# Later loads of q and v, and two more batches mixed by seven block products, in an attention and MLP-mixer kernel on one core

## The chip, the core and the metric

The kernel runs on one core of a Trainium2 chip. TensorE (PE in the profile) does matmuls and transposes into PSUM; VectorE (DVE), ScalarE (ACT) and GpSimd (POOL) work elementwise; SyncE (SP) issues most of the transfers. Each engine works through its own queue in program order and waits on semaphores for the others. The metric is the device time of one execution in microseconds, less is better; several executions are timed and the median is given.

## What is computed

Linear attention with the feature map phi(x) = elu(x) + 1, followed by one block of an MLP mixer, for 8 batches, 8 heads, 576 positions and 64 features per head. Inputs and output are float32.

```python
q_p, k_p = phi(q), phi(k)                      # phi(x) = min(exp(x), max(x + 1, 1))
kv  = einsum('bhsd,bhse->bhde', k_p, v)
z   = sum(k_p, axis=2)
x   = (q_p @ kv) / (q_p @ z + 1e-6)            # laid out as (batch, 576, 512)
h   = relu(x^T @ w_tok1) @ w_tok2              # mixing of positions, 576 -> 256 -> 576
u   = x + h^T
out = u + relu(u @ w_ch1) @ w_ch2              # mixing of channels, 512 -> 1536 -> 512
```

## The kernel before

Everything is in bfloat16 between the float32 inputs and the float32 output. Positions of a batch are split into four blocks of 128 and a tail of 64; the tails of two batches are worked on together. The order of all instructions is written by hand. It is a pipeline over batches: while batch n is mixed by channel on TensorE, batch n + 1 goes through attention and the mixing of positions, and batch n + 2 is loaded and mapped by phi. This text calls the loop pass for batch n **stage n**.

A stage is a list `big` of TensorE's pieces and a list `fill` of everything else. `put(s, fn, ...)` says that `fn` is emitted right after piece number s; what has the same s comes in the order of the `put`s. So s sets the place of an operation in the queue of its engine, and with that all that stands behind it there.

In stages 2 to 6, `big` has these pieces:

- pieces 0 to 11, the first mixing of batch n (u @ w_ch1). `mm3(n, mc)` computes one block of 128 of the 1536 hidden channels for all 512 positions: four matmuls of 512 columns (L543), and ScalarE applies relu (L550) into `cr`. There are twelve blocks. Where n is in `MIXED`, four of the twelve blocks (4, 5, 10 and 11) are computed together by a Winograd form of block multiplication, `mix_one` (L713): seven products i = 1 to 7, each four matmuls of 256 columns (L723). Their left sides are sums of weights made once (`swc`), their right sides four differences of blocks of u made by VectorE in `u_sums` (L700, into `tuc`, which is the space of `crt`). Three products are copied out of PSUM by ScalarE (L731), one has relu by ScalarE (L729), and three are finished by VectorE, which adds a copied part and clips at zero (`add_relu`, L531). The pieces are then four `mm3`, three pieces with one product and one `mm3`, products 7, 2 and 3, the last `mm3`, and product 4. `both` and `m3x` write this list.
- in stage 3 only, three pieces for the tails of batches 2 and 3 (`mm3_tail`, L557), which read `uTt`.
- fourteen pieces of the second mixing, `pair_product` (L823), also by seven products, in the order 1, 2, 6, 5, 7, 3, 4, two pieces each. They use three PSUM banks: X (products 1, 6, 7, 4), Y (5, 3) and Z (2). VectorE makes their sums of rows (`row_sums`, L666), ScalarE copies banks out in between (`pair_copy`, L828), VectorE adds u to a bank (`pair_end`, L832), and GpSimd adds the copied part and writes the result to memory.

`b0` is the number of the first of these fourteen pieces: 12, and 15 in stage 3. The rest of a stage lies between:

- `nd` for batch n + 1 at piece 1: 40 small matmuls of `qT` with `kv` (L261), then about 4.1 us of VectorE, which divides them (L270 to L289) and leaves x. `mm1` at 7 (L312) and `mm2a`, `mm2b` at 13 and b0 + 3 (L325) are the mixing of positions; VectorE's L337 makes u from them.
- `uta` and `utb` (`utr_dma`, L521): two transposes by DMA from SyncE's queue, u to `uT`, which the first mixing of batch n + 1 reads from its first matmul on. `utt` (L526) does it for a pair of tails, `ut` to `uTt`.
- phi for batch n + 2: `phi_exp` (L151, ScalarE), `phi_add` (L157, VectorE) and `phi_end` (L165, VectorE), each in two halves, once for k and once for q. `qtr_dma` (L221) then transposes q's map by two DMAs to `qT`, which `nd` of the next stage reads.
- `vcast` (L176), `kv` (L191) for batch n + 2, and `load_all(n + 3, ...)` (L132): loads of 576 KB each, two for q, two for k and two for v, into the one buffer that these have. A load waits in SyncE's queue until the old content has been read, and what stands behind it there waits too.

Stage 1 is written out by itself ahead of the loop, with pieces 0 to 31: the first mixing of batch 1 and of the tails of batches 0 and 1, its second mixing by `pair_product`, and last the second mixing of those tails (L583). In it the loads of batch 4 stand at 16 (q) and 25 (k, v), the transposes of u of batch 2 at 19 and 24.

Of the kernel before, what the change touches and what calls it, by code (L numbers as in the profile page):

```python
# [19 lines left out]
def kernel(  # L20
# [22 lines left out]
    B, H, S, D = q.shape  # L43
# [586 lines left out]
    def bf(nm, b, i):  # L630
        t = raw[nm, b].rearrange("p j f -> p (j f)").bitcast(BF16)
        return t[:, 1536 * i:1536 * (i + 1)]
# [64 lines left out]
    def u_sums(which, tu=tu, b=1):  # L697
# [5 lines left out]
    tuc = [t.rearrange("p (r j c) -> p r j c", r=2, j=2) for t in [  # L703
        crt.rearrange("p k s -> p (k s)")[:, 512 * i:512 * (i + 1)] for i in range(3)] + [
        bf("q", 1, 2)[:, 1024:1536]]]
# [159 lines left out]
    def m4s(n):  # L865
        return [lambda i=i, j=j: pair_product(n, i, j) for i in ORDER for j in range(2)]
# [133 lines left out]
    def steps(n):  # L1000

        out_ = [("kv", lambda: kv(n, range(2)))] if n < 2 else []
        if n == 1:
            puts = [nc.scalar.copy, nc.vector.tensor_copy if n == 1 else nc.scalar.copy]
            out_ += [(f"qt{c}", lambda c=c: qtr(n, c, puts[c])) for c in range(2)]
        for i, rs in enumerate(([0, 1], [2, 3], [4])) if n < 2 else ():
            for g in range(2):
                out_.append((f"nd{i}{g}", lambda g=g, rs=rs: nd(n, g, rs)))
        if n > 1:
            out_.append(("nd", lambda: nd_all(n)))  # L1010
        out_.append(("mm1", lambda: mm1(n)))
        if n > 1:
            out_ += [("mm2a", lambda: mm2(n, [0, 1])), ("mm2b", lambda: mm2(n, [2, 3]))]
            if n % 2:
                out_.append(("mm2t", lambda: mm2_tails(n // 2)))
            out_ += [("uta", lambda: utr_dma(n, [0, 1])), ("utb", lambda: utr_dma(n, [2, 3]))]
            if n % 2:
                out_.append(("utt", lambda: utr_tail_dma(n // 2)))
        return out_

    def run(bigs, fill):
        for i, big in enumerate(bigs):
            big()
            for s, fn in fill:
                if s == i:
                    fn()
        for s, fn in fill:
            assert s < len(bigs)
# [57 lines left out]
    put = lambda s, fn, *a: fill.append((s, lambda: fn(*a)))  # L1086
# [42 lines left out]
    put(24, todo["mm2b"])  # L1129
    put(24, todo["utb"])  # L1130
    put(24, pair_end, 1, "Z", 0, 0, 0)
    put(16, load_all, 4, "q")
    put(25, load_all, 4, "kv")
    put(26, pair_end, 1, "Y", 0, 1, 1)
    put(28, pair_end, 1, "X", 1, 0)
    put(28, pair_put, 1)
# [1 line left out]
    put(28, kv, 3, range(2))  # L1138
    run(big, sorted(fill, key=lambda e: e[0]))

    MIXED = (2, 3, 6)
    for n in range(2, B - 1):
        p, b = divmod(n, 2)
        tail = int(n == 3)
        mix = n in MIXED
        big = (m3x if mix else m3)(n) + m3t * tail + m4s(n) + m4(p, [8]) * tail
        b0 = 12 + 3 * tail
        todo = dict(steps(n + 1))
        fill = []
        put = lambda s, fn, *a: fill.append((s, lambda: fn(*a)))  # L1150
        at = lambda s, *nms: [put(s, todo.pop(nm)) for nm in nms if nm in todo]

        def phi_at(nm, ex, ad, en):
            for g in range(2):
                if ex is not None:
                    put(ex[g], phi_exp, nm, n + 2, 2 * g, 2)
            for g in range(2):
                put(ad[g], phi_add, nm, n + 2, 2 * g, 2)
                put(en[g], phi_end, nm, n + 2, 2 * g, 2)

        at(1, "nd")
        if n + 2 < B:
            if n > 3:
                phi_at("k", None, (2, 2), (3, 4))
                put(5, load_all, n + 3, "k")
            nm = "k" if n == 3 else "q"
            if mix:
                for which in (3, 4):
                    put(3, u_sums, which, tuc, b)
            if not mix:  # L1170
                phi_at(nm, (7, 7), (8, 9), (9, 10))
            else:
                for g in range(2):
                    put(3, phi_add, nm, n + 2, 2 * g, 2)
                    put(7, phi_exp, nm, n + 2, 2 * g, 2)
            put(10, *((qtr_dma, n + 2) if n != 3 else (load_all, n + 3, "k")))
            if n == 2:
                for g in range(2):
                    put(13, phi_add, "k", n + 2, 2 * g, 2)
        at(7, "mm1")  # L1180
        for s, k0 in ((7 if mix else 11, 0), (11 if mix else 12, 3)):
            for w in (1, 2):
                put(s, row_sums, n, w, k0, 3)
        if mix and n + 2 < B:
            for g in range(2):
                put(7 + 2 * g, phi_end, nm, n + 2, 2 * g, 2)
        if mix:
            for which in (1, 2):
                put(0, u_sums, which, tuc, b)
        if n == 3:  # L1190
            phi_at("q", (12, 13), (13, 13), (14, 14))
            put(15, qtr_dma, n + 2)
        at(13, "mm2a", "uta")
        put(14, row_sums, n, 3, 0, KH)
        put(b0 + 1, pair_copy, 0)
        if n == 2:
            for g in range(2):
                put(b0 + 1, phi_exp, "k", n + 2, 2 * g, 2)
                put(b0 + 2, phi_end, "k", n + 2, 2 * g, 2)
            put(b0 + 4, load_all, n + 3, "k")  # L1200
        at(b0 + 3 - tail, "mm2b", "utb")
        put(b0 + 4 - tail, row_sums, n, 4, 0, KH)
        put(b0 + 4 - tail, pair_end, n, "Z", 0, 0, 0)
        put(b0 + 5, pair_copy, 1)
        if n + 2 < B:
            for g in range(2):
                put(b0 + (5 if n == 2 else 2) + g, vcast, n + 2, g)
        put(b0 + 7, load_all, n + 3, "qv")
        put(b0 + 7, pair_copy, 2)
        if n > 2 and n + 3 < B:  # L1210
            put(b0 + 8, k_exp, n + 3)
        put(b0 + 9, pair_end, n, "X", 1, 1, 2)
        if n == B - 2:
            at(b0 + 6, "mm2t", "utt")
        at(b0 + 9, "mm2t")
        if n + 2 < B:
            put(b0 + 9, kv, n + 2, range(2))
        at(b0 + 9, "utt")
        put(b0 + 11, pair_end, n, "Y", 0, 1, 1)
        if n == B - 2:  # L1220
            for which in (3, 4):
                put(3, u_sums, which, tuc, b)
            put(1, first_sum)
            for which in range(1, 5):
                if which > 1:
                    put((3, 3, b0 + 2)[which - 2], first_sums, which)
                put(b0 + 10, u_sums, which)
        else:
            put(b0 + 13, pair_end, n, "X", 1, 0)
            put(b0 + 13, pair_put, n)  # L1230
        assert not todo, todo
        run(big, sorted(fill, key=lambda e: e[0]))
# [31 lines left out]
```

## Time and profile before

| | us |
|---|---|
| median of 6 executions | 252.09 |
| lowest, highest | 250.09, 254.03 |
| profiled execution | 253.14 |
| its span, first to last instruction | 251.4 |
| stage 2 (85.42 to 112.48 us of the span) | 27.1 |
| stage 3 (112.48 to 143.45) | 31.0 |
| stage 4 (143.45 to 169.11) | 25.7 |
| stage 5 (169.11 to 194.21) | 25.1 |
| stage 6 (194.21 to 218.76) | 24.6 |

A stage is counted here from its first `mm3` to that of the next. Stages 2, 3 and 6 have the seven products in their first mixing; stages 4 and 5 have not. Stage 3 has the tails of batches 2 and 3 besides.

How busy each engine is in stages 4, 5 and 6 (the columns are the stretch and its length, then busy time and number of instructions of PE, the weight loads, DVE, ACT and POOL, then the clock granted to TensorE as a share of its full speed, the mean busy share of the DMA engines, and GB/s):

```profile
143.45:169.11 25.66, 25.55 (x266) 15.96 (x266) 19.80 (x31) 16.63 (x25) 4.03 (x5) 1.00 0.76 214
169.11:194.21 25.10, 25.00 (x261) 15.84 (x262) 18.52 (x29) 14.63 (x23) 5.12 (x6) 1.00 0.53 142
194.21:218.76 24.55, 24.45 (x207) 16.54 (x207) 21.28 (x35) 9.71 (x17) 8.47 (x11) 1.00 0.34 70
```

TensorE is hardly idle in any of them. VectorE is next. Busy times of matmuls overlap, [...]so that the time between two starts is what counts: eight `mm3` matmuls of 512 columns take 1.73 us in the chain of waits, four of 256 columns 0.44 us.

### The profile page before, as it was taken

The numbers are of one execution on the slowest core, as the hardware profiler recorded it, in microseconds if no ns is written. First come the engines' busy times: TensorE is split into PE (matmuls) and PEld (weight loads), VectorE is DVE, ScalarE is ACT, GpSimd is POOL, SyncE is SP. The second block draws the span as 40 slices with busy tenths as digits, with TensorE's granted clock in tenths as the row PEclk, the third lists the DMA queues.
The fourth block names the chain that finished last, engine by engine and source line by source line (L and its number), as shares of the span: only waits on it lengthen the run. The fifth ranks groups of instructions, "written<-read, shape, count | busy, mean of one in ns | idle before, by whom it ended". The sixth has DMA issues, their size and how long they took to land.

```text
span 251.4 us, 5964 instructions
## 1 busy us (share of the span) xinstructions
PE 240.3 (96%) x2432; PEld 159.3 (63%) x2454; DVE 190.9 (76%) x330; ACT 139.4 (55%) x224; POOL 70.6 (28%) x84
## 2 busy tenths in 40 slices
PE   7899999999999699999989999999999999999994
PEld 3584455555877256775578644774478567888673
DVE  5954778897999579988986379857974888956853
ACT  4664791579765058646877268555952652175100
POOL 9770030496504500052002610052005800440000
PEclk9999999999999889999999999999999999999998
DMA  6999999999529990569959876799162602352036
GB/s 243 258 203 255 357 256 339 332 261 313 220 50 254 261 389 4 132 161 348 305 189 172 330 254 192 134 262 315 32 138 44 143 24 44 63 106 63 4 83 167
DMA packets 49771, 48.39 MB, mean 193 GB/s; under 512 B 30032, under 2 KB 35536, under 8 KB 49744
## 3 DMA queue, kind: packets, MB, share of 16 engines
q1 hardware_dynamic: 41648, 35.00, 47.3%
q0 software_dynamic: 7472, 12.22, 21.9%
q10 hardware_dynamic: 624, 0.79, 1.1%
q8 instruction: 19, 0.31, 0.5%
q14 instruction: 8, 0.07, 0.1%
HBM read 35.85 MB, written 9.44 MB: 180 GB/s over the span
## 4 chain that ended last, share of the span: by engine, by line
PE 59%; DMA 7%; DVE 3%; issue 1%; DVEq 0%
PE ps L823 18%; PE ps L543 15%; DMA uTt<-ut 5%; PE ps L751 4%; PE ps L777 4%; PE ps L312 3%; PE ps L325 3%; PE ps L723 2%; DMA uT<-u 2%; PE ps L570 2%; PE ps L592 2%; PE ps L261 1%; PE ps L191 1%; PE ps L557 1%; PE ps L583 1%
## 5 line engine op out<-in xcount | busy, mean ns | idle before, releaser
L543 PE MATMUL ps<-uT,wc 128*128 128x512 bf16 x284 | 67.7, 384 | 2.5 <-DMA uT<-u 2.1
L550 ACT ACTIVATE cr<-ps 128x512 bf16<-128x512 f32 x67 | 39.1, 600 | 37.9 <-PE ps L543 37.5
L543 PEld LDWEIGHTS <-wc 128*128 128x128 bf16 x288 | 27.5, 98 | 32.6 <-DMA uT<-u 2.6
L834 POOL TENSOR_TENSOR obuf<-obuf,q_raw 128x512 f32<-128x512 f32 x6 | 7.6, 1269 | 96.0 <-DVE obuf L832 63.4
L823 PE MATMUL ps<-k_raw,v_raw 128*128 128x256 bf16 x216 | 24.9, 273 | 0.0
L832 DVE TENSOR_TENSOR obuf<-ps,u 128x512 f32<-128x512 f32 x24 | 16.2, 686 | 10.5 <-PE ps L823 8.9
L823 PEld LDWEIGHTS <-cr 128*128 128x128 bf16 x216 | 21.0, 98 | 4.1
L823 PEld LDWEIGHTS <-v_raw 128*128 128x128 bf16 x216 | 21.1, 98 | 3.9 <-issue 0.4
L151 ACT ACTIVATE e<-q_raw 128x1152 bf16<-128x1152 f32 x16 | 18.3, 1162 | 7.2 <-DVE den L241 5.1
L151 ACT ACTIVATE e<-k_raw 128x1152 bf16<-128x1152 f32 x16 | 18.2, 1164 | 3.6 <-DMA k_raw<-in_k_dram 3.5
L823 PE MATMUL ps<-wc,cr 128*128 128x256 bf16 x144 | 17.7, 273 | 0.0
L666 DVE TENSOR_TENSOR v_raw<-cr 128x768 bf16<-128x768 bf16 (+2 forms) x24 | 14.8, 618 | 3.6 <-ACT cr L729 2.1
L276 DVE TENSOR_TENSOR x<-ps,dens 128x768 bf16<-128x768 f32 x18 | 17.2, 954 | 0.4
L337 DVE TENSOR_TENSOR u<-ps,x 128x1024 bf16<-128x1024 f32 x12 | 14.6, 1220 | 2.1 <-PE ps L325 1.9
L312 PE MATMUL ps<-x,w 128*128 128x512 bf16 x49 | 13.4, 379 | 0.3
L176 ACT CAST vs<-v_raw 128x1152 bf16<-128x1152 f32 x12 | 13.5, 1163 | 0.0
L157 DVE TENSOR_SCALAR y<-k_raw 128x1152 bf16<-128x1152 f32 x16 | 11.7, 761 | 2.2 <-DMA k_raw<-in_k_dram 2.2
L165 DVE TENSOR_TENSOR qp<-e,y 128x1152 bf16<-128x1152 bf16 x16 | 11.9, 755 | 1.0 <-ACT e L151 0.3
L157 DVE TENSOR_SCALAR y<-q_raw 128x1152 bf16<-128x1152 f32 x16 | 12.3, 783 | 0.1
L325 PE MATMUL ps<-ar,w2p 128*128 128x512 bf16 x44 | 11.8, 379 | 0.3
L834 POOL TENSOR_TENSOR obuf<-obuf,part 128x512 f32<-128x512 f32 x6 | 7.6, 1274 | 15.8 <-DVE obuf L832 15.8
L165 DVE TENSOR_TENSOR kp<-e,y 128x1152 bf16<-128x1152 bf16 x16 | 11.7, 750 | 0.5 <-ACT e L151 0.4
(178 smaller groups left out, 432.1 us busy)
## 6 DMA issues: line engine op xcount, KB each, us to landing
k_raw<-in_k_dram SPq DMA_DIRECT2D x16, 576.0 KB, 6.6
q_raw<-in_q_dram SPq DMA_DIRECT2D x16, 576.0 KB, 6.0
v_raw<-in_v_dram SPq DMA_DIRECT2D x14, 576.0 KB, 9.3
out_dram<-obuf POOLq DMA_DIRECT2D x12, 512.0 KB, 6.6
wc<-in_moe_w_ch_dram POOLq DMA_DIRECT2D x8, 384.0 KB, 10.2
out_dram<-obuf POOLq DMA_DIRECT2D x4, 256.0 KB, 5.5
cr<-in_v_dram POOLq DMA_DIRECT2D x2, 288.0 KB, 7.9
out_dram<-obuf POOLq DMA_DIRECT2D x4, 128.0 KB, 7.7
```

Of the source, the lines that this page charges most:

```text
L151: nc.scalar.activation(out=e, in_=f, func=AF.Exp)
L157: nc.vector.tensor_scalar(out=y, in0=f, scalar1=1.0, scalar2=1.0, op0=ALU.add, op1=ALU.max)
L165: live["phi"] = nc.vector.tensor_tensor(out=dst.transpose([0, 2, 1, 3]), in0=e.rearrange("p (i t d) -> p i t d", i=nj, t=T), in1=y.rearran ...
L276: nc.vector.tensor_tensor(out=xv[:, :, rc0:rc0 + 3], in0=v_[m][:, :, k0:k0 + 6, 0:D].rearrange("p i (q a) d -> p i q a d", a=2), in1=den.r ...
L312: nc.tensor.matmul(out=ps[:, mt], lhsT=w1t[:, b, ms] if r == R else w1[:, r, ms], rhs=x[b][:, r, :], start=(r == 0), stop=(r == R))
L325: nc.tensor.matmul(out=ps[:, i], lhsT=w2v(kt, r, b), rhs=ar[b][:, kt, :], start=(kt == 0), stop=(kt == NT - 1 and not add))
L543: nc.tensor.matmul(out=ps, lhsT=wc1[:, kj, 128 * mc:128 * mc + 128], rhs=uTj[b][:, kj] if n < 2 else uT[b][:, :, kj], start=(kj == 0), sto ...
L550: nc.scalar.activation(out=cr[b][:, mc, :], in_=ps, func=AF.Relu)
L666: nc.vector.tensor_tensor(out=s_[which - 1][:, ks], in0=x_, in1=y_, op=op)
L823: nc.tensor.matmul(out=live[tile_][:, j], lhsT=lhs[:, k_], rhs=rhs[:, k_], start=(first and j == 0 and k_ == 0), stop=(k_ == KH - 1), skip ...
L832: nc.vector.tensor_tensor(out=o, in0=live[tile_], in1=u[n % 2][:, d::2, HC[c]], op=ALU.add)
L834: nc.gpsimd.tensor_tensor(out=o, in0=o, in1=part[i], op=ALU.add)
```

## The change

Three places change.

- In stage 1 the load of q of batch 4 moves from piece 16 to piece 25, ahead of k and v of that batch; all six transfers now stand behind both transposes of u of batch 2 in SyncE's queue.
- In stage 2 the loads of q and v of batch 5 move from piece 19 to piece 21, behind the transpose of the tails of batches 2 and 3. In the other stages they stay.
- `MIXED` gets batches 4 and 5. In their stages the four blocks of the first mixing are computed by seven products; VectorE makes the four differences of u, two at piece 0 and two at piece 2, ahead of k's map, and the first sums of rows move to pieces 7 and 11, as in the other stages with products. In both stages q's `phi_add` and `phi_end` move from pieces 7 to 10 to pieces 17 and 18, and `qtr_dma` from 10 to 18, in SyncE's queue now behind the transposes of u and still ahead of the loads at 19. q's `phi_exp` stays at 7, k's map at 2 to 4.

For stages 2, 3 and 6 the new conditions give the same order as before, but for the load in stage 2.

```diff
@@ -1129,8 +1129,7 @@
-    put(16, load_all, 4, "q")
-    put(25, load_all, 4, "kv")
+    put(25, load_all, 4, "qkv")
@@ -1138,7 +1137,7 @@
-    MIXED = (2, 3, 6)
+    MIXED = (2, 3, 4, 5, 6)
@@ -1159,29 +1158,32 @@
         at(1, "nd")
+        if mix and 3 < n < B - 2:
+            for which in (3, 4):
+                put(2, u_sums, which, tuc, b)
         if n + 2 < B:
             if n > 3:
                 phi_at("k", None, (2, 2), (3, 4))
                 put(5, load_all, n + 3, "k")
             nm = "k" if n == 3 else "q"
-            if mix:
+            if n > 3:
+                phi_at(nm, (7, 7), (b0 + 5, b0 + 5), (b0 + 6, b0 + 6))
+            else:
                 for which in (3, 4):
                     put(3, u_sums, which, tuc, b)
-            if not mix:
-                phi_at(nm, (7, 7), (8, 9), (9, 10))
-            else:
                 for g in range(2):
                     put(3, phi_add, nm, n + 2, 2 * g, 2)
                     put(7, phi_exp, nm, n + 2, 2 * g, 2)
-            put(10, *((qtr_dma, n + 2) if n != 3 else (load_all, n + 3, "k")))
+            put(b0 + 6 if n > 3 else 10,
+                *((qtr_dma, n + 2) if n != 3 else (load_all, n + 3, "k")))
...
-        for s, k0 in ((7 if mix else 11, 0), (11 if mix else 12, 3)):
+        for s, k0 in ((7, 0), (11, 3)):
             for w in (1, 2):
                 put(s, row_sums, n, w, k0, 3)
-        if mix and n + 2 < B:
+        if n < 4:
             for g in range(2):
                 put(7 + 2 * g, phi_end, nm, n + 2, 2 * g, 2)
...
-        put(b0 + 7, load_all, n + 3, "qv")
+        if n != 2:
+            put(b0 + 7, load_all, n + 3, "qv")
...
         at(b0 + 9, "utt")
+        if n == 2:
+            put(b0 + 9, load_all, n + 3, "qv")
```

## The prediction

> **What bounds the kernel now.** I read the shares of busy time first, then the table of who waited for whom on TensorE, then the chain of waits in order of time, and last windows and timelines around the places found.
>
> ```profile
> PE 240.3 (96%) x2432; PEld 159.3 (63%) x2454; DVE 190.9 (76%) x330; ACT 139.4 (55%) x224; POOL 70.6 (28%) x84
> ```
>
> TensorE is busy for 240.3 of 251.4 us, so time goes only with matmuls, with TensorE's few idle stretches, or with a slow clock. In the waits (us in total, times, longest) only two of its idle stretches lie behind the first 20 us:
>
> ```profile
> PE ps L543 <- DMA uT<-u: 2.1, 1, 2.1
> PE ps L557 <- DMA uTt<-ut: 0.8, 1, 0.8
> ```
>
> The first stands at the seam of stage 1 and stage 2 ("stage n" is the loop in which batch n is mixed by channel). The chain in order of time (start, us, what) shows it with its sequel, and stage 5 for comparison:
>
> ```profile
> 79.31 6.06 DMA uT<-u
> 85.38 0.05 issue
> 85.42 3.10 PE ps L543 x8
> 88.52 1.12 PE ps L261 x27
> ...
> 182.50 1.31 PE ps L823 x12
> ...
> 194.21 1.73 PE ps L543 x8
> 195.94 0.72 PE ps L261 x40
> ```
>
> Stage 1's last matmul ends at 83.27; the transposes of u of batch 2 land at 85.4. Then the same eight matmuls that take 1.73 us at 194.21 take 3.10. The one-microsecond windows give the reason in their PEclk column (the one ahead of the last two):
>
> ```profile
> 84.40:85.40 1.00, 0.00 (x0) 0.00 (x0) 0.00 (x0) 0.00 (x0) 0.91 (x2) 1.00 0.98 272
> 87.40:88.40 1.00, 1.00 (x3) 0.15 (x1) 0.00 (x0) 0.05 (x1) 0.00 (x0) 0.50 1.01 336
> 89.40:90.40 1.00, 1.00 (x18) 0.52 (x13) 0.81 (x3) 0.00 (x0) 0.00 (x0) 1.00 1.02 411
> ```
>
> The clock is granted at half from about 86.0 to 89.4. SyncE's queue says why the transposes were late: 1.15 MB of q of batch 4 are issued right ahead of them.
>
> ```profile
> 75.55 1.16 SPq L132 DMA_DIRECT2D q_raw<-in_q_dram  x2
> 76.80 5.01 SPq L521 DMA_TRANSPOSE uT<-u  x2
> ```
>
> Each of these two transposes needs 2.5 us to issue and the second 6.1 to land; over all twelve the minimum and median are 3.0 and 3.1.
>
> [...]
>
> **The change, part by part.** My base is the profiled execution: 253.14 us, of which the span is 251.4.
>
> *Loads of batch 4.* All three now follow the transposes. The second transpose can issue at 79.31 as before (VectorE's L337 ends then) and lands 3.1 us later, at 82.4, 0.9 ahead of TensorE's 83.27. The wait goes: -2.15. With it goes the idleness that halved the clock. From its start to its first L823, stage 2 takes 14.72 us (85.42 to 100.14), stage 6, with the same matmuls, 13.00 (194.21 to 207.21): -1.72. Bounds: 0 to -2.15 and 0 to -1.72. What the move costs: q of batch 4 issues at about 80.6 instead of 75.6 and, at the 4.2 to 6.0 us of such loads, has landed by 87.5. VectorE reads it once nd (6.5 us into a stage) and two differences (0.8) are done, at 90.6. That cover of 3 us hides it; k and v are wanted 8 us later still.
>
> *q and v of batch 5* now follow the tail's transpose in stage 2. That issues when its data are there (about 111) behind k's 1.15 MB alone and lands, at the 6.1 us of its like, at 117 instead of 126.3; TensorE wants it at 125.5: -0.83. q and v move back about 1.2 us (one issue); q landed near 121, and its map is at 126 to 128, so 0.
>
> *Seven products in stages 4 and 5.* Sixteen 512-column matmuls (3.46 us at 216 ns) become 28 of 256 (3.05 at 109). Read from whole stages: 13.39 us from stage 5's start to its first L823 (169.11 to 182.50), 13.00 in stage 6, which has the products: -0.39 each, -0.78 together. ScalarE keeps 12 operations per stage, of 0.58 to 0.60 us each. VectorE gains four differences at 0.42 and three add-and-clip at 0.69, 3.75 us: 23.6 of 25.3 us in stage 4, 22.3 of 24.7 in stage 5. Two of the differences fit into its 1.65 us of idleness ahead of nd. The rest is tight but has a pattern: stage 2 has the products and the map of q, and its TensorE has no wait. With k's map (2.7 us) done in one piece ahead of the first add-and-clip, that ends 10.5 us into the stage and the next two at 12.2 and 12.85; the products that read them start at 13.0 and 13.65. I take 0; from nothing up to 0.5 per stage.
>
> *q's map later.* Its four operations move behind this stretch (start, us; stage 5 starts at 169.11):
>
> ```profile
> 186.88 1.23 DVE L337 TENSOR_TENSOR u<-ps,x 128x1024 bf16<-128x1024 f32 x1
> 188.03 0.95 DVE L666 TENSOR_TENSOR q_raw<-cr,v_raw 128x1536 bf16<-128x1536 bf16 x1
> 188.89 0.68 DVE L832 TENSOR_TENSOR obuf<-ps,u 128x512 f32<-128x512 f32 x1
> 190.88 0.69 DVE L832 TENSOR_TENSOR obuf<-ps,u 128x512 f32<-128x512 f32 x1 [1.31 <-PE ps L823]
> ```
>
> Their L337 waits for TensorE, which is 0.4 earlier, so the first L832 ends at 189.5 - 169.1 - 0.4 = 20.0 into the stage. The map takes 4 x 0.67 and ends at 22.75. Only then can SyncE issue the two transposes of qT, 1.4 us each, the second landing 3.6 later: 22.8 + 1.4 + 3.6 = 27.8. Before, they were issued 12 us into the stage (155.74), so nothing waited. Now nd of the next stage reads them at stage length plus 1.73: 25.27 + 1.73 = 27.0 after stage 4, 24.71 + 1.73 = 26.45 after stage 5. New waits: +0.75 and +1.3 (bounds 0.4 to 1.2 and 0.9 to 1.75, from the 4.9 to 5.4 us between the map's end and the landing in stages 2 and 3). Behind the map, the L832 that frees bank X ends at about 23.4; product 4 writes X at 23.8 in stage 4, 23.3 in stage 5: +0.1. SyncE's queue behind qT: q and v of batch 7 issue 5 us later, at 25.6; q lands 6 us on, 7 into stage 5, its exp is wanted at 8.3: 0. v is wanted at 15, the tail's transpose only in the last block: 0. GpSimd's adds shift by under 1 us and nobody waits for them.
>
> **Sum:** -2.15 - 1.72 - 0.83 - 0.78 + 0.75 + 1.3 + 0.1 = -3.33, from 253.14 to **249.8**. The profiled execution is 1.05 above the median of 252.09, and the half clock may be missing in some executions (they range over 3.9 us); the same sum from the median gives 248.8. I take **249.5**.
>
> **Rivals.**
> (a) *qT in time*: if VectorE is earlier than I think, only -5.5 remains: about 247.5. Against it: the map can't begin before the L832 at 20.0. 12%.
> (b) *One of the new waits halves the clock again*, +1.72: 251.2. For it: 2.15 us did. Against it: the 0.83 us at 125.5 left the clock at 1.00. 18%.
> (c) *Slower*: qT lands late. Its transposes share the DMA engines with q and v of batch 7 right behind them and with two 512 KB stores. The two waits sum to twice the landing minus 5.05 us; they eat up the whole gain from a landing of 5.3 us on. At the 6.1 that transposes needed behind q, the waits are 7.15, and both exceed 2.15, so twice 1.72 for the clock: 253.14 - 5.48 + 10.6 = 258.3. For it: 6.1 and 12.1 occur. Against it: in both cases the loads were ahead in the queue, here they are behind. 12%.
> (d) *The first transposes stay slow* for a reason other than q ahead of them: 253.14 - 1.61 + 2.15 = 253.7. Against it: of the other ten transposes of u nine landed in 3.0 to 3.6 us, and the one of 5.3 (at 134.8) was issued right behind those of qT, which here are done by 77.6. 8%.
>
> **Numbers.** About 1% (2.5 us) is what a measurement here can tell from no change; 1% faster is 249.57. My forecast has 50%, on its own from 248.2 to 250.8, with a little over half below 249.57. Faster: 0.30 from it, 0.12 from (a), 0.02 from (b): 0.44. Same: 0.20 + 0.16 + 0.08 = 0.44. Slower: (c), 0.12. The range reaches down past (a), to 247.2, and up past (b), to 252.4; it leaves out (c) and (d).
>
> **What would show it.** Right: SyncE issues q of batch 4 behind the two transposes, no wait of L543 for uT, PEclk at 1.00 throughout stage 2, no wait of L557; L261 waiting for DMA qT, 0.75 and 1.3 us, at the starts of stages 5 and 6; 28 matmuls of L723 in stages 4 and 5. Wrong: waits for qT over 2 us or PEclk of 0.5 behind them; waits of L823 for VectorE's L531 or L832, which would say that VectorE, not the transposes, bounds stages 4 and 5; or a wait of L157 for q of batch 4.

## The result and the profile after

| | before | after |
|---|---|---|
| median of the runs compared, us | 250.83 (70 runs) | 252.85 (33 runs) |
| lowest, highest, us | 248.11, 254.38 | 251.68, 255.04 |
| ratio, 95% interval | | 1.0092 [1.0076, 1.0108] |
| profiled execution, us | 253.14 | 252.83 |
| its span, us | 251.4 | 251.1 |

The kernel is 0.9% slower, and 252.85 lies above the forecast range, while the two profiled executions differ by 0.3 us the other way. Of 115 executions of the kernel before that ran beside the experiments below, 16 have a mean granted clock below 0.9945 and take some 2 us longer, and the profiled execution of before (0.990) is one of that kind.

TensorE in the profile after does less work and is idle for longer; the first line is that of busy times in the page, the others are from the table of who waited for whom (us in total, times, longest):

```profile
PE 237.0 (94%) x2456; PEld 160.8 (64%) x2478; DVE 199.3 (79%) x344; ACT 139.1 (55%) x224; POOL 70.9 (28%) x84
```

```profile
PE ps L261 <- DMA qT<-qp: 2.5, 2, 1.3
PE ps L823 <- DVE obuf L832: 1.6, 2, 1.1
...
PE ps L543 <- DMA uT<-u: 0.7, 1, 0.7
```

The wait for the tail's transpose is gone, the wait for u's transposes is down from 2.1 to 0.7 us. Two new ones have come, twice each: for q's transposes in front of nd, and for VectorE's add in front of the last product. Stages 4, 5 and 6 (columns as in the table before) show the bill:

```profile
139.10:165.04 25.94, 25.31 (x277) 17.15 (x278) 23.33 (x38) 16.46 (x25) 3.99 (x4) 1.00 0.51 152
165.04:192.41 27.37, 24.93 (x274) 17.09 (x274) 23.55 (x37) 14.45 (x23) 5.57 (x6) 1.00 0.61 172
192.41:218.37 25.96, 24.63 (x207) 16.61 (x207) 21.58 (x35) 9.71 (x17) 8.74 (x11) 1.00 0.39 83
```

They take 79.3 us, against 75.3 before and 76.7 by the prediction: PE's busy time shrank in stages 4 and 5, but each of the three stages grew. Where the time goes in stage 4 is seen in VectorE's timeline (start, us, instruction):

```profile
158.49 0.68 DVE L832 TENSOR_TENSOR obuf<-ps,u 128x512 f32<-128x512 f32 x1
159.09 2.49 DVE L157 TENSOR_SCALAR y<-q_raw 128x1152 bf16<-128x1152 f32 x2
161.50 1.41 DVE L165 TENSOR_TENSOR qp<-e,y 128x1152 bf16<-128x1152 bf16 x2
162.84 0.68 DVE L832 TENSOR_TENSOR obuf<-ps,u 128x512 f32<-128x512 f32 x1
```

q's map begins 20.0 us into the stage, to the tenth where the prediction put it. But its two L157 take 2.49 us instead of 1.42. GpSimd's timeline shows what stands beside them:

```profile
159.31 1.65 POOL L834 TENSOR_TENSOR obuf<-obuf,q_raw 128x512 f32<-128x512 f32 x1 [18.11 <-DVE obuf L832]
```

This add of the copied part to Z is released by the very L832 that the map follows. The kernel before has the same add at this place, with nothing of VectorE's map beside it; in its stage 5, which starts at 169.11, it is this line:

```profile
189.71 1.27 POOL L834 TENSOR_TENSOR obuf<-obuf,q_raw 128x512 f32<-128x512 f32 x1 [18.02 <-ACT w L828]
```

In the profile after, the add of stage 4 runs until 160.96, and the second L157 (the list of that line's instructions in this window gives their durations as least, median, most) takes 1.83 us:

```profile
L157 DVE TENSOR_SCALAR y<-q_raw x2: 750/1288/1827, 159.1 to 159.8; 128x1152 bf16<-128x1152 f32 x2
```

The chain of waits then goes on to the next stage: the end of the map, q's second transpose, nd. (SyncE issues the first transpose at 162.94, as soon as the map has ended; the L832 in the chain only runs meanwhile.)

```profile
162.91 0.61 DVE obuf L832
163.53 0.70 SPq L221
164.23 0.05 issue
164.28 3.83 DMA qT<-qp
168.12 0.05 issue
168.16 0.76 PE ps L261 x38
```

### The profile page after: what moved, and what is told of

It is laid out like the page before. It is cut to its first block, busy times and chain, and to the rows that moved or that the text cites. A ratio compares the mean times of both kernels' runs of the same rounds, so it can differ in the third digit from the quotient of the medians.

```text
span 251.1 us, 6016 instructions
## 1 busy us (share of the span) xinstructions
PE 237.0 (94%) x2456; PEld 160.8 (64%) x2478; DVE 199.3 (79%) x344; ACT 139.1 (55%) x224; POOL 70.9 (28%) x84
## 4 chain that ended last, share of the span: by engine, by line
PE 57%; DVE 6%; DMA 5%; issue 2%; ACT 1%; SPq 0%; DVEq 0%; ACTq 0%
PE ps L823 14%; PE ps L543 13%; PE ps L723 6%; PE ps L312 4%; PE ps L751 4%; PE ps L777 4%; PE ps L325 3%; DMA qT<-qp 3%; PE ps L570 2%; PE ps L592 2%; DMA uT<-u 2%; DVE y L157 2%; PE ps L261 1%; DVE obuf L832 1%; PE ps L557 1%
## 5 line engine op out<-in xcount | busy, mean ns | idle before, releaser
L543 PE MATMUL ps<-uT,wc 128*128 128x512 bf16 x252 | 60.2, 379 | 1.1 <-DMA uT<-u 0.7
L550 ACT ACTIVATE cr<-ps 128x512 bf16<-128x512 f32 x59 | 34.5, 600 | 39.4 <-PE ps L543 39.2
L543 PEld LDWEIGHTS <-wc 128*128 128x128 bf16 x256 | 24.2, 98 | 25.5 <-DMA uT<-u 1.2
L834 POOL TENSOR_TENSOR obuf<-obuf,q_raw 128x512 f32<-128x512 f32 x6 | 8.4, 1396 | 93.2 <-DVE obuf L832 59.1
L823 PE MATMUL ps<-k_raw,v_raw 128*128 128x256 bf16 x216 | 24.9, 273 | 0.0
L823 PEld LDWEIGHTS <-cr 128*128 128x128 bf16 x216 | 21.0, 98 | 5.6 <-issue 1.9
L823 PEld LDWEIGHTS <-v_raw 128*128 128x128 bf16 x216 | 21.0, 98 | 3.9 <-issue 0.4
L151 ACT ACTIVATE e<-q_raw 128x1152 bf16<-128x1152 f32 x16 | 18.3, 1165 | 6.7 <-DMA q_raw<-in_q_dram 6.7
L832 DVE TENSOR_TENSOR obuf<-ps,u 128x512 f32<-128x512 f32 x24 | 16.0, 683 | 5.6 <-PE ps L823 4.0
L151 ACT ACTIVATE e<-k_raw 128x1152 bf16<-128x1152 f32 x16 | 18.2, 1165 | 3.5 <-DMA k_raw<-in_k_dram 3.4
L823 PE MATMUL ps<-wc,cr 128*128 128x256 bf16 x144 | 17.7, 273 | 0.0
L157 DVE TENSOR_SCALAR y<-q_raw 128x1152 bf16<-128x1152 f32 x16 | 14.3, 917 | 0.0
L157 DVE TENSOR_SCALAR y<-k_raw 128x1152 bf16<-128x1152 f32 x16 | 11.7, 762 | 2.1 <-DMA k_raw<-in_k_dram 2.1
L834 POOL TENSOR_TENSOR obuf<-obuf,part 128x512 f32<-128x512 f32 x6 | 7.6, 1272 | 19.7 <-DVE obuf L832 19.7
```

Of the source, the lines that this page charges most:

```text
L151: nc.scalar.activation(out=e, in_=f, func=AF.Exp)
L157: nc.vector.tensor_scalar(out=y, in0=f, scalar1=1.0, scalar2=1.0, op0=ALU.add, op1=ALU.max)
L543: nc.tensor.matmul(out=ps, lhsT=wc1[:, kj, 128 * mc:128 * mc + 128], rhs=uTj[b][:, kj] if n < 2 else uT[b][:, :, kj], start=(kj == 0), sto ...
L550: nc.scalar.activation(out=cr[b][:, mc, :], in_=ps, func=AF.Relu)
L823: nc.tensor.matmul(out=live[tile_][:, j], lhsT=lhs[:, k_], rhs=rhs[:, k_], start=(first and j == 0 and k_ == 0), stop=(k_ == KH - 1), skip ...
L832: nc.vector.tensor_tensor(out=o, in0=live[tile_], in1=u[n % 2][:, d::2, HC[c]], op=ALU.add)
```

## The experiments

All times are medians. Each ratio is to executions of the kernel before that ran in the same set, on the same chip; it is not the quotient of the medians (for e2_mix that would be 1.0115). There are four sets, and the kernel before has these medians in them: 252.33 (n0, e1, e2, e3), 250.84 (r_after, e4, e5, e6), 250.58 (e3b, e7, e8) and 250.89 (e1b). The first two sets ran on one chip, the others on two more. So ratios are to be compared, not times of different sets.

| label | what it is | us | ratio, 95% interval |
|---|---|---|---|
| n0_before | the kernel before, profiled once more | 254.07 (one execution) | |
| e1_loads | the two moves of loads alone | 249.01 | 0.9881 [0.9831, 0.9930] |
| e1b_loads | the same, on another chip | 249.11 | 0.9927 [0.9904, 0.9949] |
| e2_mix | the products with the late map alone | 255.24 | 1.0146 [1.0094, 1.0198] |
| r_after | the whole change | 253.26 | 1.0109 [1.0058, 1.0160] |
| e3_map_early | the change, map in its old places | 247.76 | 0.9842 [0.9787, 0.9897] |
| e3b_map_early | the same, on another chip | 247.83 | 0.9892 [0.9854, 0.9930] |
| e4_no_z_add | the change without GpSimd's add to Z in stages 4, 5 | 250.67 | 1.0012 [0.9975, 1.0048] |
| e5_z_behind | the change, add to Z behind the map | 250.28 | 0.9983 [0.9955, 1.0012] |
| e6_q4_only | q of batch 4 moved alone | 250.01 | 0.9981 [0.9947, 1.0014] |
| e7_qv5_only | q and v of batch 5 moved alone | 249.77 | 0.9955 [0.9927, 0.9983] |
| e8_gate | e3_map_early, the loads of batch 4 held until the transpose has landed | 250.07 | 0.9947 [0.9915, 0.9979] |

### Was the profile of before a usual one?

> The kernel before once more, for a second profile. If the half clock at the start of stage 2 belongs to every execution, PEclk is 0.5 for some 3.4 us there again and the span is near 251.4 us. If the profiled execution was out of the ordinary in this (it is 2.3 us above the median of 70), PEclk is 1.00 throughout, stage 2 takes some 25.5 us instead of 27.1, and the span is near 249.

Neither case as written. The span is 252.3 us. TensorE's waits, and two windows, during and behind the wait of L557 (PEclk is the column ahead of the last two):

```profile
PE ps L557 <- DMA uTt<-ut: 2.2, 1, 2.2
PE ps L543 <- DMA uT<-u: 1.5, 1, 1.5
```

```profile
123.30:125.30 2.00, 0.00 (x0) 0.00 (x0) 1.50 (x4) 0.64 (x2) 0.00 (x0) 1.00 0.98 61
127.00:129.00 2.00, 2.00 (x16) 1.45 (x14) 0.00 (x0) 1.94 (x4) 0.00 (x0) 0.50 0.38 147
```

Stage 2 took 25.5 us this time, its first eight matmuls of L543 1.90 us, at full clock; the half clock came behind the other wait, in stage 3. So which wait is long, and whether the clock falls behind it, changes from execution to execution. One profile gives a pair (2.1 and 0.8), not the pair.

### The two halves of the change

```diff
 e1_loads, on the kernel before
-    put(16, load_all, 4, "q")
-    put(25, load_all, 4, "kv")
+    put(25, load_all, 4, "qkv")
...
+        if n != 2:
             put(b0 + 7, load_all, n + 3, "qv")
...
         at(b0 + 9, "utt")
+        if n == 2:
+            put(b0 + 9, load_all, n + 3, "qv")
```

> Only the two moves of loads. If they save what the profile after shows (0.7 instead of 2.1 us of waiting for uT, no 0.8 us of waiting for uTt), the time is some 2 us below before (ratio near 0.992), with stages 4 and 5 as before at 25.7 and 25.1 us. If their gain was only the half clock of one odd execution, the ratio is 1.000.

e2_mix is the change with these lines as before.

> Only the seven products in stages 4 and 5 with q's map late; loads as before. If stages 4 to 6 lose by themselves what the profile after shows (79.3 against 75.3 us), the time is 3.9 us above before (ratio near 1.016) and loads and products add up to the whole change. If the loads of batch 4 or 5 in their new places cause part of that loss, it is less.

The loads gain 1.2% here, and in their profile TensorE waits neither for uT nor for uTt. The products with the late map lose 1.5%, near the 1.6% that stages 4 to 6 of the profile after give. Then the whole change on the same chip, in the next set:

> The whole change once more, on the chip that its parts run on. If its two halves act independently, its ratio is that of the loads alone times that of the products alone, 0.9881 x 1.0146 = 1.0025, within the intervals; if the loads of batch 4 or 5 in their new places also hurt stages 4 and 5, it is above.

It gave 1.0109 [1.0058, 1.0160], in agreement with the 1.0092 of the result; 1.0025 lies outside both, but each of its two factors is itself uncertain by 0.5%. What differs between the sets is the kernel before: 252.33 beside the parts, with the low clock in 5 of 11 executions, and 250.84 beside the whole, with the low clock in 1 of 34. An estimate from medians across the two sets: against 250.84 the loads give 0.9927 and the products 1.0175, together 1.0101. The loads were measured a second time:

> Only the two moves of loads, once more. The first time they gave 0.988, but on a chip whose runs of the kernel before had a low clock in 5 of 11 cases (median 252.3); the single moves gave 0.998 and 0.9955 where that is rare (median 250.6 to 250.8). If the moves' gain is largely what that slow clock costs, it is near 0.9935 on a chip of the second kind and 0.988 on one of the first; if it is the same everywhere, 0.988.

0.9927 [0.9904, 0.9949], where 6 of 27 executions of before had the low clock. The moved loads themselves took the same both times, 249.0 and 249.1 us. So the two ratios differ through the kernel before; that it is the chip which decides, as the expectation has it, is not shown, because one chip gave both 5 of 11 and 1 of 34. 0.9927 x 1.0146 is 1.0072, and the interval of e2_mix is 0.5% wide to each side, so the halves are consistent with acting independently.

### Which load does it

```diff
 e6_q4_only, on the kernel before
-    put(16, load_all, 4, "q")
-    put(25, load_all, 4, "kv")
+    put(25, load_all, 4, "qkv")
```

> The kernel before with only q of batch 4 moved behind the transposes of u. If each of the two moves takes away its own wait, this one has no wait of L543 for uT and still one of L557 for uTt, and about half of the gain of both (ratio 0.988): near 0.994. If all of the gain is here, it is 0.988; if none, 1.000.

```profile
PE ps L557 <- DMA uTt<-ut: 2.0, 1, 2.0
...
PE ps L543 <- DMA uT<-u: 0.7, 1, 0.7
```

Less than expected, 0.998. The first wait shrank, and 2.0 us of waiting for the tail's transpose (it landed 12.6 us after its issue) came behind it. The 32 matmuls of L557 behind that took 2.51 us (1.79 in e7_qv5_only), and the mean granted clock of this profile is 0.993. That the second wait is long because the first is short is not shown: with q in its old place the tail cost 0.8 us in before, 2.2 in n0_before and 0.6 in e2_mix. e7_qv5_only is the other move alone.

> The kernel before with only q and v of batch 5 moved behind the tail's transpose. No wait of L557 for uTt is left; the wait of L543 for uT stays at 1.5 to 2.1 us. The other move alone gave 0.998 because TensorE then came to the tail's transpose earlier and waited 2.0 us there. This one has nothing behind it to give its gain back to: 0.990 to 0.995. If the two moves were equal, 0.998.

0.9955, at the edge of what was expected, and the waits as expected: none for uTt, 2.1 us for uT, behind which eight matmuls of L543 took 3.24 us (1.90 in n0_before; the mean granted clock of this profile is 0.992). The intervals of the two single moves overlap, and 0.9981 x 0.9955 = 0.9936 agrees with the 0.9927 of both moves. So the runs do not show that one move gains more than the other, nor that either needs the other.

### Is it the late map?

```diff
 e3_map_early, on the change
-                phi_at(nm, (7, 7), (b0 + 5, b0 + 5), (b0 + 6, b0 + 6))
+                phi_at(nm, (7, 7), (8, 9), (9, 10))
...
-            put(b0 + 6 if n > 3 else 10,
+            put(10,
                 *((qtr_dma, n + 2) if n != 3 else (load_all, n + 3, "k")))
```

> The change with q's map and its transposes back in their old places (pieces 7 to 10). If the late map is what costs, no wait for qT and none of L823 for VectorE is left, stages 4 and 5 take 25.3 and 24.7 us, and the time falls by 4.7 us from 252.85 to about 248.1 (ratio 0.989). If VectorE is simply overloaded by the seven products, it is late in these stages here too: waits of L823 or L325 for VectorE of a us or more per stage, and the time stays above that of the loads alone.

> The change with q's map in its old places once more (it was 4.6 us below the kernel before, ratio 0.984), as the standard for the next one on the same chip: again below 0.99, stages 4 and 5 at 25.3 and 24.8 us.

247.8 both times, against the 248.1 expected, and 0.984 and 0.989 of before. Stages 4 and 5 of the second run:

```profile
138.41:163.67 25.26, 25.16 (x277) 17.14 (x278) 22.67 (x38) 16.46 (x25) 3.98 (x5) 1.00 0.69 210
163.67:188.41 24.74, 24.64 (x273) 17.02 (x274) 21.47 (x36) 14.46 (x23) 5.07 (x6) 1.00 0.71 163
```

25.3 and 24.7, as expected. VectorE is busy for 90% and 87% of them and not late: TensorE waits for it nowhere in stages 4 and 5. The rival, that the products overload VectorE wherever the map stands, is out. Against e1_loads (25.66 and 25.10) the products themselves save 0.40 and 0.36 us. This version beats both kernels.

### What makes the map so expensive late

```diff
 e4_no_z_add, on the change
-        put(b0 + 4 - tail, pair_end, n, "Z", 0, 0, 0)
+        put(b0 + 4 - tail, pair_end, n, "Z", 0, 0, None if n in (4, 5) else 0)
```

> The change, but in stages 4 and 5 GpSimd's add of the copied part to Z is left out, so that part of the result of batches 4 and 5 lacks a term; VectorE's and TensorE's work is the same. If that add, which runs beside q's phi_add, is what makes the pair take 2.49 us, it takes 1.42 here, the waits of L823 for VectorE (0.5 and 1.1) fall below 0.2 and the time is about 2 us below the whole change. If something else slows L157 (ScalarE's exp of k, which starts beside it, or a transfer), it stays near 2.5 us and the time stays too.

VectorE's timeline, and the waits of TensorE:

```profile
157.56 0.68 DVE L832 TENSOR_TENSOR obuf<-ps,u 128x512 f32<-128x512 f32 x1
158.16 1.42 DVE L157 TENSOR_SCALAR y<-q_raw 128x1152 bf16<-128x1152 f32 x2
159.49 1.42 DVE L165 TENSOR_TENSOR qp<-e,y 128x1152 bf16<-128x1152 bf16 x2
160.83 0.68 DVE L832 TENSOR_TENSOR obuf<-ps,u 128x512 f32<-128x512 f32 x1
```

```profile
PE ps L261 <- DMA qT<-qp: 1.9, 2, 1.2
```

1.42 us, no wait of L823 left, and 250.67 against 253.26 on the same chip: one add on GpSimd, for which TensorE never waits, was worth 2.6 us. In the profiles of the change and of this run, 2.2 us of that are waits for X and qT. ScalarE's exp of k is still there, and in the profile of before an L157 with an exp beside it (at 29.04 us, L151 from 29.10) takes 0.76 us: it is not that. In the profile of the change, stage 4, L834 is released while the first L157 is running, which keeps its 0.75 us; L834 takes 1.65 us instead of 1.27, and the second L157 loses 1.08 us (1.83 instead of 0.75) and ends 0.62 us after L834 has. Two L157 in the profile of before look the same: at 32.99 (1.05 us, beside L923 on GpSimd) and at 54.08 (0.90 us, beside L653), each ending about 0.6 us after that instruction of GpSimd. That the add is the cause is shown by leaving it out; by what it slows L157 is not shown.

e5_z_behind keeps all the work, takes the add away from beside the map, and with VectorE's part of it behind the map lets the map start 0.6 us earlier:

```diff
-        put(b0 + 4 - tail, pair_end, n, "Z", 0, 0, 0)
+        put(b0 + (6 if n in (4, 5) else 4 - tail), pair_end, n, "Z", 0, 0, 0)
```

> The change, with VectorE's add to bank Z moved behind q's map in stages 4 and 5. By my account the map then starts 0.6 us earlier and has no GpSimd beside it, ends 22.1 us into the stage instead of 23.8, and the waits shrink to 0.15 and 0.65 us for qT and 0.1 for X, 3.2 us less than the whole change. If the lateness of the map is not what counts, the time stays at the whole change's.

VectorE's timeline, and the waits of TensorE:

```profile
158.66 1.42 DVE L157 TENSOR_SCALAR y<-q_raw 128x1152 bf16<-128x1152 f32 x2
```

```profile
PE ps L261 <- DMA qT<-qp: 1.7, 2, 1.3
```

250.28, 3.0 us less than the whole change, with L157 at 1.42 and no wait for X. The waits for qT are 0.33 and 1.34. The second is double what I expected: in stage 5 the second transpose issues 2.35 us behind the first instead of 1.4, because the first takes 2.3 us to issue. A packet of the kind described in the next part runs during that issue (from 187.88 to 188.80); that it is the cause was not tested.

### Why u's transpose lands late

```diff
 e8_gate, on e3_map_early
-        nc.sync.dma_start_transpose(
+        live["utr"] = nc.sync.dma_start_transpose(
...
-    put(25, load_all, 4, "qkv")
+    put(25, lambda: load("q", 4, 0, live["utr"]))
+    put(25, load, "q", 4, 1)
+    put(25, load_all, 4, "kv")
```

> The same, and the first load of q of batch 4 waits until the second transpose of u of batch 2 has landed, not only until it is issued. If the loads right behind that transpose are what makes it land after 4.6 instead of 3.1 us in the whole change, it lands after 3.1 to 3.3 here in every execution and no wait of L543 for uT is left: up to 0.8 us below the one before it where that one has the wait. If the 4.6 have another cause, nothing changes. Should q now be late for its map, L157 waits for it and stage 2 is longer than 25.5 us.

The expectation failed on both counts. The transpose landed after 4.6 us with nothing behind it: in the window from 81.5 us on, the DMA engines are busy for 0.12 of the time and the transpose still lands at 83.9. And q is late now, as VectorE's timeline shows:

```profile
93.00 0.76 DVE L157 TENSOR_SCALAR y<-q_raw 128x1152 bf16<-128x1152 f32 x1 [1.73 <-DMA q_raw<-in_q_dram]
94.42 0.76 DVE L157 TENSOR_SCALAR y<-q_raw 128x1152 bf16<-128x1152 f32 x1 [0.66 <-DMA q_raw<-in_q_dram]
```

Its 22 runs fall into two groups, 8 from 247.1 to 248.0 and 14 from 249.9 to 250.8. In the profiles without q ahead of it, this transpose lands either after 3.1 us (e1, e1b, e3, e3b, e4) or after 4.6 to 4.8 (the change twice, e5, e6, e8); nothing lies between. The loads behind it do not decide.

The kept traces show what goes with the late landings. The profiles of before and after each have 19 packets of 16 KB in a DMA queue of their own, which the page calls q8, kind "instruction". In e8_gate one of them falls into the window from 78 to 84 us:

```profile
q8 instruction: 1, 0.02, 1.0%
```

In each of the five profiles with 4.6 to 4.8 us such a packet starts between 81.56 and 81.88 us and takes 0.94 to 0.97 us, and the transpose's last packets start where it ends, 3.6 us after the issue. In each of the five with 3.1 us none starts between 74 and 88 us, and the last packets start 2.6 us after the issue. So 1.0 of the 1.5 us is accounted for. The 6.1 us of the kernel before, which the prediction put down to q alone, has such a packet in it too (at 83.19). Of all 168 transposes of u in the fourteen profiles, 28 landed after more than 4 us: 24 have such a packet in their time, and the other four stand right behind q of batch 4. It does not delay every transpose that it meets: twelve others had one begin in their last 0.6 us and still landed after 3.1 to 3.2 us. No run moved these packets, so the cause is read from the traces and not tested.

## Why the prediction was wrong, point by point

The forecast was 249.5 within 247.2 to 252.4, from the sum -3.33. The measured 252.85 is above the range, and the kernel became slower instead of faster.

- **The base.** The sum was made against the profiled execution. Its -1.72 for the half clock is about right for that execution (stage 2 took 25.5 us in n0_before instead of 27.1) but is no gain to the median, whose executions mostly have full clock (a mean of 0.9945 or more in 99 of 115). The prediction said so as a doubt and took only 0.3 us off for it.
- **Loads of batch 4, -2.15.** The direction was right; the term was oversized. In the profile after 0.7 us of waiting stayed, because the landing was 4.6 us, not 3.1; where it was 3.1 (e1, e1b, e3, e3b, e4) the wait went altogether. Alone the move gives 0.2%, with an interval that includes nothing (e6_q4_only). One reading was wrong without bearing on the sum: only the second transpose took 2.5 us to issue, the first took 1.24.
- **Loads of batch 5, -0.83.** Right: the wait is gone, and q and v came in time. Both moves together gain 0.7% to 1.2%.
- **Seven products, -0.78, VectorE in time.** Right: 0.76 in e3b_map_early, with no wait for VectorE.
- **q's map later: "The map takes 4 x 0.67 and ends at 22.75".** This is the step that failed. The start, 20.0, was right; the end was 23.8 (162.91 less 139.10), because the two L157 took 2.49 us instead of 1.42. L157's price came from places where GpSimd is idle, and the profile of before had GpSimd's L834 in just the slot to which the map went (189.71 to 190.98 in stage 5). "GpSimd's adds shift by under 1 us and nobody waits for them" looked only at who waits for the add, not at who runs beside it. From this follow 1.6 us of waiting for X instead of 0.1 and 2.5 us for qT instead of 2.05. Without the add (e4_no_z_add) the map of stage 4 ends 22.74 into it, qT lands at 27.8, and the waits are 0.77 and 1.2: the predicted 22.75, 27.8, 0.75 and 1.3. With this step right the change would still only have equalled the kernel before (1.0012); the gain that is missing then lies in the base and in the loads.
- **The rivals.** (a), qT in time, did not happen. (b), another half clock, did not: 1.3 us of waiting left it at 1.00. (c) came nearest in its sign but not in its mechanism: qT landed after 3.5 to 3.8 us as forecast, its source was late. (d) is half true in the profile after: the transpose landed after 4.6 us, between the 3.1 assumed and the 6.1 of before, and what goes with that is the packet of q8.

In one line: loads 0.9927, and on top of them the late map's waits, 4.1 us, less the products' 0.8; without GpSimd beside the map it equals the kernel before (1.0012 in e4_no_z_add, 0.9983 in e5_z_behind, which keeps all the work), with the map in its old place it is 1.1% to 1.6% faster.

## What to carry to other kernels

When an instruction of VectorE is moved, look at what GpSimd does in the new place and not only at VectorE's own queue: an add that nobody waits for cost 2.6 us here. Price the moved instruction from a place with the same neighbours. And before a wait is counted as a gain, see whether the profiled execution is like the median one. When a transfer lands late, look at all DMA queues in that window, not only at the one that it stands in.

## What the runs showed of the hardware

- The granted clock was 0.50 behind idle stretches of TensorE of 2.15 us (before, from 86.0 to 89.4 us) and 2.23 us (n0_before, in the window from 127 to 129 us). Behind 2.0 us (e6_q4_only) 32 matmuls of L557 took 2.51 us, against 1.79, and behind 2.1 us (e7_qv5_only) eight of L543 took 3.24, against 1.90; the mean granted clocks of these two profiles are 0.993 and 0.992. Behind 1.5 us (n0_before's first wait) eight of L543 took 1.90 us, and the clock was 1.00 behind 0.7 us (the change's wait for uT, windows from 83 to 88 us) and behind its waits for qT of up to 1.3 us (stages 5 and 6).
- An fp32 add of 128x512 on GpSimd (1.27 us alone, in before) and two L157 on VectorE (1.42 us alone, in e4_no_z_add) that overlap take 1.65 and 2.49 us (in after, stage 4).
- The same DMA transpose of 128x1024 in bfloat16, with its queue empty ahead of it, lands after 3.1 or after 4.6 to 4.8 us. The loads behind it do not decide which (e8_gate). In the five late cases, and in none of the five early ones, a 16 KB packet of queue q8 runs when its last packets are due, and they start where that packet ends.
